# A longformer attention and softplus-MLP kernel: the planner's rules for queue, ring, port and fetch, and a new order

## The chip, the cores and the metric

The kernel runs on one core of a Trainium2 chip. The metric is device time in microseconds (us). Five engines work side by side and meet only at semaphores: TensorE (PE: matmuls; PEld is its weight load), VectorE (DVE), ScalarE (ACT), GpSimd (POOL) and SyncE (SP, which only issues transfers here). GpSimd issues transfers too, on a queue of its own.

## What is computed

Attention over 8 batches of 8 heads, 576 positions and 64 features, where a position sees its neighbours within 32 and 8 global positions; then, on the 4608 rows of 512 features, a layer of 2048 with softplus and a layer back to 512.

```python
scores = scale * np.matmul(q, k.transpose(0, 1, 3, 2))
mask = np.abs(pos[:, None] - pos[None, :]) <= 32
mask = mask | is_global[:, None] | is_global[None, :]
scores = np.where(mask, scores, -1e9)
attn = np.exp(scores - np.max(scores, axis=-1, keepdims=True))
attn = attn / (np.sum(attn, axis=-1, keepdims=True) + 1e-09)
x = np.matmul(attn, v).transpose(0, 2, 1, 3).reshape(4608, 512)
h = x @ w_in                      # 512 x 2048
g = np.maximum(h, 0.0) + np.log1p(np.exp(-np.abs(h)))
out = g @ w_out                   # 2048 x 512
```

## The kernel before

**The work.** The 4608 rows are nine tiles of 512. A tile is four groups of 128 positions ("pairs" n in the code). For each group TensorE makes the scores `s` (L1105), DVE adds the mask and takes the maximum (`st`, `m`, L1109 and L1122), GpSimd subtracts it (`st`, L1128), ACT takes the exponential (L1145), DVE sums and inverts (`sm`, `rs`, L1152 and L1154), GpSimd multiplies (`pn`, L1160), DVE transposes (`pt`, L1169), and TensorE multiplies with the values (`xo`, L1271). The first four groups take a shorter path, whose mask TensorE adds. The result is copied to `xT`, and the two layers follow: `h` (L1308, with weights `win`), softplus to `g` (L1314, ACT), and `o` (L1319, with weights `wout`), copied to `osb` and stored. Global rows of a batch go a way of their own: scores `sg` (L1003), maximum `gm` and `gnb` on DVE, exponential `pg` on ACT (L1015), transposed `pgt` (L1019, L1020), `ov` (L1029) on TensorE, then `odd`, `grs` and `vg`, which `xo` needs. `fill` copies a batch's global keys into `kx` (L755, `kx<-qkg`). The transposes of a later batch are `qx` (L859) and `kx` (L863). The first tile is cut into pieces of 128, 256 and 128 rows, the second into 128 and 384.

**The order.** Nothing in the program is in the order in which the code names it. Every step is a job with a cost on each engine that may do it, and `_Order.run` takes the jobs in the order that the table `ORDER` lists (a number is five times the job's number, plus its engine). The table so fixes which engine does a job and what stands in an engine's queue before what. The planner's own times decide two things more: how many filler matmuls `warm` (L762) are put on TensorE where it is planned to wait in the first 34 us (`keep`), and which PSUM bank a result takes. Each engine works off its queue in that order, and a step at the head that waits holds all behind it.

**The queues.** SP issues the loads of q and k, GpSimd those of `vb` (rounded values, 16 transfers), `win` (two to each of four tiles) and `wout` (four). SP's loads for batch 1 stand behind a tiny transfer, `trail<-win` (L789), which waits until the third tile of `win` has landed; those for batch 2 stand behind `trail<-wout`. GpSimd reads one element of the second half of batch 1's k (`seen`, L1454) before it issues `wout`, and issues batch 1's `vb` behind that.

**What the planner knows.** `stall` models TensorE's instructions as blocks of 256, asked for some 282 instructions before they are needed; `comes` says when such a block arrives. A job with `port` isn't put on DVE while GpSimd works on data, nor the other way round.

Of the kernel before, what the change touches and what calls it, by code (L numbers as in the profile page):

```python
# [19 lines left out]
class _Order:  # L20
# [20 lines left out]
    QUIET = 5000  # L41
    NEAR = 150

    def comes(self, here):

        t = here + self.QUIET
        for mine, start, moves, j in self.dma:
            if mine == "POOL" and j["at"] <= here + 300:
                t = max(t, min(j["end"] + 2300, here + 9300))
        return t  # L50

    def stall(self, t, took, ins):

        held, n = 0, self.issued
        asked, need, due, last = self.fetch
        due = list(due)
        while n + ins >= min(asked, need):
            at = min(asked, need)
            here = t + held + took * max(at - n, 0) / max(ins, 1)
            if at == asked:  # L60
                last = max(self.comes(here), last + self.FETCH)
                due.append(last)
                asked += self.BLOCK
            else:
                held += max(0, due.pop(0) - here)
                need += self.BLOCK
        return held, (asked, need, due, last)

    def add(self, cost, emit, deps=(), rank=5, opens=(), uses=(), table=None, moves=0, array=128, urgent=False, ins=None, late=0, hold=0, behind=(), lead=0, port=False):

        job = dict(cost=cost, emit=emit, deps=[d for d in deps if d is not None], rank=rank, opens=list(opens),
                   table=table, moves=moves, array=array, urgent=urgent, ins=ins, late=late, hold=hold, lead=lead, port=port, behind=[d for d in behind if d is not None], n=len(self.jobs), at=None, end=None)
# [91 lines left out]

    def size(self, j):
        return j["ins"] or 2
# [38 lines left out]
    def run(self, free):  # L205
# [13 lines left out]
        self.mine, self.other = [], []  # L219
        self.fetch, self.issued = (self.ASK, self.NEED, [], 0), 0  # L220
        while ready:
# [6 lines left out]
            for j in self.picked(ready):  # L228
# [6 lines left out]
                for e in j["cost"] if not self.given else [self.given[0][1]]:  # L235
# [7 lines left out]
                    elif e == "DVE" and j["port"]:  # L243
                        for a, z in self.other[-4:]:
                            if a <= t + 100 and z > t:
                                t = self.freed(z) if (a, z) == self.other[-1] else z
                    elif e == "POOL" and not self.issue(j):
# [46 lines left out]
            j["on"] = e  # L294
            order.append(j)
# [17 lines left out]
def kernel(  # L313
# [455 lines left out]
    T = {}  # L769
# [725 lines left out]
```

## Time and profile before

| | |
|---|---|
| median of 3 runs | 329.61 us (329.25 to 332.41) |
| the profiled execution | 331.38 us, of which the span of its instructions is 329.7 us |
| granted TensorE clock, mean | 0.99 |
| filler matmuls in the program | 34 |
| jobs on ACT, DVE, GpSimd | 364, 313, 143 |

A row of a timeline gives the start and length of an instruction or of several alike, the engine, the line, the operation with its tiles, and in brackets how long the engine had been idle before it and what ended that. "PEclk" is the granted clock of TensorE as a share of full speed. "issue" names a wait that nothing in the profile explains.

### The profile page before, as it was taken

What the parts mean: (1) busy time and instruction counts of PE and PEld (TensorE: products, weight loads), DVE (VectorE), ACT (ScalarE), POOL (GpSimd) and SP (SyncE); (2) the same over time, 40 slices, a digit from 0 to 9 for tenths busy, and PEclk for the clock granted to TensorE, in tenths of its full rate; (3) what the DMA queues carried; (4) which work ended last, traced back from release to release, by engine and by line L of the source; (5) the groups of instructions that cost most, each with busy time, mean ns of one, the idle gap of its engine ahead of it and who ended that gap; (6) DMA issues with size and microseconds to landing.
All of it is one profiled execution on the core that took longest, in us unless ns stands there. A gap on an engine that the chain in (4) does not pass through costs nothing.

```text
span 329.7 us, 11617 instructions
## 1 busy us (share of the span) xinstructions
PE 313.2 (95%) x5018; PEld 172.4 (52%) x5061; DVE 230.2 (70%) x410; ACT 224.9 (68%) x458; POOL 199.7 (61%) x180
## 2 busy tenths in 40 slices
PE   8879999699999998999999999999999999999996
PEld 3448974266557554544454455444544544454453
DVE  7876786974899999988985787599749727450000
ACT  7969844577589897398648972877569746934432
POOL 8984737977399377578768952949585604740000
PEclk9998999989999999999999999999999999999999
DMA  8999999995988999979990997403320002001002
GB/s 210 170 178 242 176 196 141 189 216 137 155 129 140 198 179 180 174 158 143 180 207 34 188 151 161 105 2 74 130 97 0 36 2 97 1 34 66 32 16 111
DMA packets 168651, 41.50 MB, mean 126 GB/s; under 512 B 153114, under 2 KB 165658, under 8 KB 168602
## 3 DMA queue, kind: packets, MB, share of 16 engines
q1 hardware_dynamic: 151048, 25.96, 44.7%
q0 software_dynamic: 15680, 11.67, 20.3%
q10 hardware_dynamic: 1874, 3.15, 2.5%
q8 instruction: 39, 0.64, 0.8%
q14 instruction: 10, 0.08, 0.1%
HBM read 36.70 MB, written 9.44 MB: 140 GB/s over the span
## 4 chain that ended last, share of the span: by engine, by line
PE 80%; DMA 9%; DVE 4%; issue 2%; POOL 2%; ACT 2%; SPq 0%
PE h L1308 34%; PE o L1319 33%; DMA stage<-in_k_dram 5%; PE xo L1271 4%; DMA wout<-in_moe_w_out_dram 4%; PE s L1105 3%; PE ov L1029 2%; POOL st L1128 1%; ACT st L1141 1%; PE pick L919 1%; PE warm L762 1%; PE sg L1003 1%; DVE sm L1152 1%; DVE kx L755 1%; POOL wout L1375 1%
## 5 line engine op out<-in xcount | busy, mean ns | idle before, releaser
L1308 PE MATMUL h<-xT,win 128*128 128x512 bf16 (+3 forms) x823 | 136.3, 314 | 1.2 <-issue 0.5
L1319 PE MATMUL o<-wout,g 128*128 128x512 bf16 (+1 forms) x563 | 131.0, 375 | 2.8 <-issue 2.4
L1314 ACT ACTIVATE g<-h 128x512 bf16<-128x512 f32 (+3 forms) x208 | 85.3, 481 | 37.5 <-PE h L1308 36.1
L1308 PEld LDWEIGHTS <-win 128*128 128x128 bf16 x832 | 70.7, 98 | 56.0 <-issue 1.2
L1160 POOL TENSOR_TENSOR pn<-st,rs 128x1024 bf16<-128x1024 f32 (+1 forms) x39 | 67.9, 1746 | 42.5 <-DVE rs L1154 38.8
L1319 PEld LDWEIGHTS <-g 128*128 128x128 bf16 x592 | 56.4, 98 | 62.0 <-issue 2.0
L1128 POOL TENSOR_TENSOR st<-st,m 128x1024 f32<-128x1024 f32 x32 | 60.3, 1897 | 24.7 <-DVE m L1122 23.9
L1109 DVE TENSOR_TENSOR st<-s,mask 128x512 f32<-128x512 f32 x64 | 41.1, 678 | 13.3 <-PE s L1105 13.3
L1152 DVE TENSOR_REDUCE sm<-st 128x8 f32<-128x1024 f32 x32 | 38.3, 1198 | 11.5 <-ACT st L1145 11.2
L1122 DVE TENSOR_REDUCE m<-st 128x8 f32<-128x1024 f32 x32 | 38.1, 1204 | 0.2
L1145 ACT ACTIVATE st<-st 128x1024 f32<-128x1024 f32 x32 | 32.9, 1055 | 5.2 <-POOL st L1128 5.0
L755 ACT COPY osb<-o 128x512 f32<-128x512 f32 (+1 forms) x26 | 14.9, 574 | 23.9 <-PE o L1319 21.6
L1169 DVE STREAM_TRANSPOSE pt<-pn 128x512 int32<-128x512 int32 x36 | 24.7, 690 | 2.8 <-POOL pn L1160 2.8
L755 DVE CAST xT<-xo 128x512 bf16<-128x512 f32 (+3 forms) x28 | 13.4, 524 | 15.9 <-PE xo L1271 15.8
L755 ACT CAST xT<-xo 128x512 bf16<-128x512 f32 (+3 forms) x24 | 9.8, 454 | 15.9 <-PE xo L1271 15.3
L1314 ACT ACT_TABLE_LOAD x13 | 16.7, 1283 | 3.0 <-PE h L1308 2.8
L1105 PE MATMUL s<-kx,qx 64*32 64x128 bf16 x1152 | 14.5, 220 | 2.4 <-DVE kx L863 1.3
L1105 PEld LDWEIGHTS <-qx 64*32 64x32 bf16 x1152 | 10.5, 90 | 10.4 <-issue 8.1
L1145 ACT ACT_TABLE_LOAD x12 | 15.4, 1283 | 0.6 <-ACT osb L755 0.4
L477 POOL DMA_DIRECT2D vb<-in_v_dram x16 | 11.1, 706 | 7.6 <-DMA wout<-in_moe_w_out_dram 7.5
L1331 POOL DMA_DIRECT2D out_dram<-osb x24 | 13.6, 569 | 3.3 <-DVE osb L755 2.2
L752 POOL TENSOR_SCALAR qk<-stage 128x1152 bf16<-128x1152 f32 (+1 forms) x9 | 12.5, 1394 | 3.6 <-PE h L1308 3.6
(129 smaller groups left out, 299.0 us busy)
## 6 DMA issues: line engine op xcount, KB each, us to landing
stage<-in_k_dram SPq DMA_DIRECT2D x48, 144.0 KB, 4.0
stage<-in_q_dram SPq DMA_DIRECT2D x48, 144.0 KB, 3.7
stage<-in_v_dram SPq DMA_DIRECT2D x48, 144.0 KB, 3.6
out_dram<-osb POOLq DMA_DIRECT2D x24, 256.0 KB, 3.0
out_dram<-osb ACTq DMA_DIRECT2D x11, 256.0 KB, 2.0
stage<-in_q_dram SPq DMA_DIRECT2D x4, 512.0 KB, 7.0
stage<-in_k_dram SPq DMA_DIRECT2D x4, 512.0 KB, 7.5
win<-in_moe_w_in_dram POOLq DMA_DIRECT2D x8, 256.0 KB, 6.5
```

The source lines that it names most:

```text
L755: {"ACT": nc.scalar.copy, "DVE": V.tensor_copy, "POOL": nc.gpsimd.tensor_copy}[e](out, in_)
L1105: nc.tensor.matmul(out=PS["s", n, g][quad(a), x, :], lhsT=qx[b % 2][rows(g), a, j * BL:(j + 1) * BL], rhs=kx[b % 2][rows(g), a, e0 * BL:(e ...
L1109: V.tensor_tensor(out=PS["st", n][:, h, :, :], in0=PS["s", n, h][:, :, :], in1=mask[:, h, j0:j0 + PB, :, :].rearrange("p j s i -> p j (s i ...
L1122: V.reduce_max(out=m[:], in_=flat(PS["st", n], h0, h1), axis=AX)
L1128: on(e).tensor_tensor(out=t, in0=t, in1=over(PS["m", n, y][:], SL * BL), op=OP.subtract)
L1145: nc.scalar.activation(out=t, in_=t, func=AF.Exp)
L1152: V.reduce_sum(out=sm[:], in_=flat(PS["st", n], h0, h1), axis=AX)
L1160: on(e).tensor_tensor(out=PS["pn", n][:, :, :, h0:h1].rearrange("p x s h -> p h x s"), in0=PS["st", n][:, h0:h1], in1=PS["rs", n, y][:].re ...
L1169: V.transpose(out=bass.AP(base.tensor, base.offset, ap=[list(base.ap[0]), [2 * STEP, PB // 2], [STEP + BL // 2, 2], [1, SL * BL]]), in_=PS ...
L1308: nc.tensor.matmul(out=h[:, :], lhsT=w_in_t[c // 4][:, kd, c % 4 * P:(c % 4 + 1) * P], rhs=PS["xT", m][:, kd, lo:hi], start=(kd == 0), sto ...
L1314: nc.scalar.activation(out=PS["g", m, c][:, lo:hi], in_=PS[key][:, lo_of(c, hi - lo)], func=AF.Softplus)
L1319: nc.tensor.matmul(out=PS["o", m, ns, a][:, :], lhsT=PS["g", m, kf][:, ns * P:(ns + 1) * P], rhs=w_out_t[kf // 4][:, kf % 4, a:z], start=( ...
```

## The change

Five rules of the planner, and with them a new table.

- Block arrival: `comes` and its constant 5000 ns go; a block asked for before a planned 13 us takes 6300 ns, then 7300, 9000, 6500, 8500 and 5000 (`SLOW`).
- GpSimd's queue: a job says how many transfers it sends (`sent`), and `ring` plans the ninth transfer not before the first of the eight ahead of it has landed.
- First transfers: batch 0's other parts are planned behind the first (`behind`), and the third and fourth tile of `win` 3700 and 3500 ns after the one before (`hold`).
- One more `port` operation: `fill` of batches 2 and later.
- `ORDER` is replaced in whole.

```diff
-    QUIET = 5000
+    SLOW = ((13000, 6300), (18000, 7300), (24000, 9000), (36000, 6500), (52000, 8500), (1e9, 5000))
-                last = max(self.comes(here), last + self.FETCH)
+                last = max(here + next(took for until, took in self.SLOW if here < until), last + self.FETCH)
+    QUEUE = 8
+    def ring(self, j, t):
+        n = len(self.sent)
+        for x in range(j["sent"]):
+            if n + x >= self.QUEUE:
+                d, back = self.sent[n + x - self.QUEUE]
+                t = max(t, d["end"] - back + 290 - 680 * x)
+        return t
...
+                    elif e == "POOL" and j["sent"]:
+                        t = self.ring(j, t)
...
-                                    rank=-1 if x else 0, hold=0, moves=2900 if x else 3500)
+                                    rank=-1 if x else 0, hold=(0, 0, 3700, 3500)[x], moves=2900 if x else 3500, sent=2)
...
-                             rank=rank - 1 if b else 0, uses=[kkey] if early else [], lead=0 if b else LEAD)
+                             rank=rank - 1 if b else 0, uses=[kkey] if early else [], lead=0 if b else LEAD, port=not early)
...
-        52, 126, 4, 57, 102, 62, 147, 65, 106, 141, 116, 201, 132, 72, 205, 217, 136, 9, 152, 212, 232, 157, 122, 14,
...
+        8820, 8826,
```

The program itself gets no rule of its own from the first four: its transfers, semaphores and instructions are the same, but for four more filler matmuls (38), and jobs that change engine. ACT has now 370 jobs, DVE 305, GpSimd 145. Lines move down by 7 or 8, so that `fill` and the other copies, L755, are now L762, and L1128 is L1136.

GpSimd's queue around the loads of `win`, before:

```order
L477 DMA vb_67<-in_v_dram 32x18x64 x8
L1371 DMA win_130<-in_moe_w_in_dram 64x4x512 x2
L1371 DMA win_131<-in_moe_w_in_dram 64x4x512 x2
L1160 TENSOR_TENSOR pn<-st,rs 128x512
L1371 DMA win_132<-in_moe_w_in_dram 64x4x512 x2
L1160 TENSOR_TENSOR pn<-st,rs 128x512 x4
L1371 DMA win_133<-in_moe_w_in_dram 64x4x512 x2
L699 COPY mask<-mask 128x2x256
```

and now, where the copy of the mask and the clearing of batch 1's tiles stand ahead of the third tile, and the fourth directly behind it; two casts of batch 0 also stand ahead of the first `vb` now:

```order
L484 DMA vb_67<-in_v_dram 32x18x64 x8
L1379 DMA win_130<-in_moe_w_in_dram 64x4x512 x2
L1379 DMA win_131<-in_moe_w_in_dram 64x4x512 x2
L706 COPY mask<-mask 128x2x256
L558 MEMSET kx_72 128x40x16
L558 MEMSET kx_72 128x4x16 x2
L558 MEMSET qkg_74 128x64
L584 MEMSET vb_68 128x18x2
L1168 TENSOR_TENSOR pn<-st,rs 128x512
L1379 DMA win_132<-in_moe_w_in_dram 64x4x512 x2
L1379 DMA win_133<-in_moe_w_in_dram 64x4x512 x2
L1168 TENSOR_TENSOR pn<-st,rs 128x512 x4
```

Around `wout`, the same queue had one cast of k shortly ahead of `seen` and nothing between `seen` and the first `wout`; now two such casts stand ahead of `seen` and two more between it and `wout`. The four `wout`, eight `vb` and four `st` behind them are as they were, in the same order. On SP's queue the loads of batch 1 were, behind the little transfer:

```order
L789 DMA trail<-win_132 1x2x1
L532 DMA stage_60<-in_q_dram 128x8x128
L532 DMA stage_61<-in_k_dram 128x8x128 x2
L532 DMA stage_60<-in_q_dram 128x8x128
L536 DMA stage_60<-in_q_dram 64x4x64 x2
```

and are now (`stage_60` is q, `stage_61` is k):

```order
L796 DMA trail<-win_132 1x2x1
L539 DMA stage_61<-in_k_dram 128x8x128 x2
L539 DMA stage_60<-in_q_dram 128x8x128 x2
L543 DMA stage_61<-in_k_dram 64x4x64 x2
L543 DMA stage_60<-in_q_dram 64x4x64 x2
```

Both of k's large loads come ahead of q's now. DVE's queue around batch 1's global row, between the last maxima of its first groups and `pgt`, before:

```order
L1122 TENSOR_REDUCE m<-st 128x8 x2
L1152 TENSOR_REDUCE sm<-st 128x8
L1154 RECIPROCAL rs<-sm 128x8
L1009 TENSOR_REDUCE gm<-sg 128x1 x2
L1010 TENSOR_REDUCE gnb<-gm 128x1
L1109 TENSOR_TENSOR st<-s,mask 128x512 x2
L1152 TENSOR_REDUCE sm<-st 128x8
L1154 RECIPROCAL rs<-sm 128x8
L1019 STREAM_TRANSPOSE pgt<-pg 128x576
L1020 TENSOR_REDUCE pgt<-own 128x18x8
```

and now, with one sum instead of two ahead of `pgt`, and `gm` ahead of both:

```order
L1130 TENSOR_REDUCE m<-st 128x8 x2
L1017 TENSOR_REDUCE gm<-sg 128x1 x2
L1018 TENSOR_REDUCE gnb<-gm 128x1
L1117 TENSOR_TENSOR st<-s,mask 128x512 x2
L1160 TENSOR_REDUCE sm<-st 128x8
L1162 RECIPROCAL rs<-sm 128x8
L1027 STREAM_TRANSPOSE pgt<-pg 128x576
L1028 TENSOR_REDUCE pgt<-own 128x18x8
```

ACT, which took three exponentials ahead of `pg`, takes two now. On TensorE thirteen fillers stand now ahead of the first `xo`, where there was none, and the four fillers between its `heat` matmuls (L768) and the first `h` are gone; up to batch 1's `ov` it has 49 `o` matmuls instead of 53. The `fill` of batch 4 moves from DVE to ACT: before, DVE had

```order
L1109 TENSOR_TENSOR st<-s,mask 128x512
L859 STREAM_TRANSPOSE qx_69<-qk 128x1152
L938 STREAM_TRANSPOSE qkg_73<-placed 128x256
L755 COPY kx_71<-qkg_73 128x40x8
L863 STREAM_TRANSPOSE kx_71<-qk 128x4x9x32
L1169 STREAM_TRANSPOSE pt<-pn 128x2x2x128
```

and now ACT has it behind a table load and an exponential:

```order
L762 COPY odd<-ov 64x129 x2
L1153 ACT_TABLE_LOAD
L1153 ACTIVATE st<-st 128x1024
L762 COPY kx_71<-qkg_73 128x40x8
L1048 ACTIVATE vg_76<-odd,grs 128x128
```

The fills of batches 2 and 5 move to ACT as well, those of 6 and 7 to DVE.

More of the change, by code (lines that the diff above doesn't have):

```diff
@@ L40 @@
     FETCH = 4000
-    QUIET = 5000
+    SLOW = ((13000, 6300), (18000, 7300), (24000, 9000), (36000, 6500), (52000, 8500), (1e9, 5000))
     NEAR = 150
[L44 to L50, printed above, removed]
     def stall(self, t, took, ins):
@@ L67, in stall, with add @@
         return held, (asked, need, due, last)
-    def add(self, cost, emit, deps=(), rank=5, opens=(), uses=(), table=None, moves=0, array=128, urgent=False, ins=None, late=0, hold=0, behind=(), lead=0, port=False):
+    def add(self, cost, emit, deps=(), rank=5, opens=(), uses=(), table=None, moves=0, array=128, urgent=False, ins=None, late=0, hold=0, behind=(), lead=0, port=False, sent=0):
         job = dict(cost=cost, emit=emit, deps=[d for d in deps if d is not None], rank=rank, opens=list(opens),
-                   table=table, moves=moves, array=array, urgent=urgent, ins=ins, late=late, hold=hold, lead=lead, port=port, behind=[d for d in behind if d is not None], n=len(self.jobs), at=None, end=None)
+                   table=table, moves=moves, array=array, urgent=urgent, ins=ins, late=late, hold=hold, lead=lead, port=port, sent=sent, behind=[d for d in behind if d is not None], n=len(self.jobs), at=None, end=None)
         self.jobs.append(job)
@@ L218, in run @@
         dma = self.dma = []
-        self.mine, self.other = [], []
+        self.mine, self.other, self.sent = [], [], []
         self.fetch, self.issued = (self.ASK, self.NEED, [], 0), 0
@@ L294, in run @@
             j["on"] = e
+            for x in range(j["sent"]):
+                self.sent.append((j, j["moves"] / 2 if x + 1 < j["sent"] else 0))
             order.append(j)
@@ L794, in add_rounded @@
             T["cast", b, 2].append(o.add({"POOL": (1360, 0)}, lambda e, c=c: load_rounded(b, c), T["cast", b, 2][-1:] or deps,
-                                         rank=-1, moves=1250, hold=0))
+                                         rank=-1, moves=1250, hold=0, sent=2))
         T["load", b, 2] = T["cast", b, 2][-1]
@@ L822, in add_parts @@
             T["part", b, w, t] = o.add({"DMA": (700 if b else 0, 0)}, emit, had(("w_in", 2)) + T["cast", 0, w] if b else [], rank=0,
-                                       moves=(1740 if b else 1830) if t < FULL else 900 if b else 670)
+                                       moves=(1740 if b else 1830) if t < FULL else 900 if b else 670,
+                                       behind=had(("part", 0, 0, 0)) if not b and x else [])
     def add_cast(b, w):
@@ L1365, in add_moe @@
             if m < OWN:
-                o.add({"POOL": (700, 2700)}, lambda e, ns=ns: store(nc.gpsimd, ns, 0, d_model), [T["oev", m, ns]], rank=-0.5, hold=0, port=2,
+                o.add({"POOL": (700, 2700)}, lambda e, ns=ns: store(nc.gpsimd, ns, 0, d_model), [T["oev", m, ns]], rank=-0.5, hold=0, port=2, sent=1,
                       uses=[("osb", m, ns)])
@@ L1456 @@
                 T["w_out", a] = o.add({"POOL": (800, 0)}, lambda e, a=a: weights_out(a),
-                                      [T["landed"], T.get(("w_out", a - 1))], rank=-1, hold=0, moves=2560)
+                                      [T["landed"], T.get(("w_out", a - 1))], rank=-1, hold=0, moves=2560, sent=1)
         for x in range(len(VALS)):
```

147 rows, old and new, of the table ORDER are left out of this document.

## The prediction

> **What bounds the kernel now.** I read the page first, then the busy time by stretches, then the timelines of the engines at the two places where TensorE stands still.
>
> ```profile
> span 329.7 us, 11617 instructions
> PE 313.2 (95%) x5018; PEld 172.4 (52%) x5061; DVE 230.2 (70%) x410; ACT 224.9 (68%) x458; POOL 199.7 (61%) x180
> ```
>
> TensorE is the bound over the whole: idle for 16.5 us of 329.7. An average hides where, so these stretches are cut at its waits:
>
> ```profile
> core 0: us, PE busy (x) PEld busy (x) DVE busy (x) ACT busy (x) POOL busy (x), PEclk, DMA share, GB/s
> 21.66:23.17 1.51, 0.26 (x7) 0.12 (x8) 1.20 (x3) 0.04 (x1) 1.34 (x2) 1.00 1.24 200
> 23.17:27.00 3.83, 3.61 (x57) 2.43 (x58) 2.17 (x6) 2.72 (x16) 1.79 (x4) 0.55 0.82 116
> 27.00:60.15 33.15, 32.48 (x645) 23.66 (x645) 24.81 (x54) 22.39 (x70) 20.68 (x27) 1.00 1.23 191
> 60.15:63.01 2.86, 0.00 (x1) 0.00 (x1) 2.79 (x6) 1.70 (x3) 2.84 (x3) 1.00 1.09 183
> 64.01:68.00 3.99, 3.66 (x72) 1.66 (x73) 2.84 (x9) 1.91 (x7) 3.84 (x4) 0.57 1.11 206
> 68.00:131.20 63.20, 61.42 (x1144) 37.73 (x1151) 55.70 (x84) 52.13 (x107) 45.06 (x32) 1.00 0.93 164
> 131.20:326.60 195.40, 192.58 (x2687) 96.50 (x2711) 121.55 (x191) 124.25 (x191) 104.01 (x71) 1.00 0.42 92
> ```
>
> After 131.2 us TensorE is busy for 192.58 of 195.40: a new order can win at most 2.8 us there. Two waits cost more than themselves, because the granted clock falls behind them, to 0.55 over 3.83 us and to 0.57 over 3.99 us, that is, (1 - 0.57) x 3.99 = 1.7 us each. The work of TensorE around the waits:
>
> ```profile
> 21.01 0.42 PE L1105 MATMUL s<-kx,qx 64*32 64x128 bf16 x32
> ...
> 23.17 0.21 PE L1271 MATMUL xo<-pt,vg 32*64 32x128 bf16 x1 [1.26 <-issue]
> ...
> 23.64 1.03 PE L768 MATMUL xo<-idle 128*128 128x256 bf16 x4
> ...
> 26.18 2.06 PE L1308 MATMUL h<-xT,win 128*128 128x128 bf16 x28
> ...
> 49.24 5.56 PE L1319 MATMUL o<-wout,g 128*128 128x512 bf16 x25
> ...
> 63.01 0.80 PE L1029 MATMUL ov<-vb,pgt 32*32 32x129 bf16 x72 [2.86 <-DVE pgt L1020]
> ...
> 66.64 0.28 PE L1271 MATMUL xo<-pt,vg 32*64 32x64 bf16 x8
> ...
> 74.05 0.38 PE L1271 MATMUL xo<-pt,vg 32*64 32x384 bf16 x8
> ```
>
> So there are three sizes to argue about: when the first `h` starts (26.18), the wait of `ov` at 60.15 with the slow clock behind it (2.86 + 1.7 = 4.6 us), and one later wait:
>
> ```profile
> 131.60 0.42 PE L1105 MATMUL s<-kx,qx 64*32 64x128 bf16 x32 [1.28 <-DVE kx L863]
> ```
>
> **The first h.** The third group of scores ended at 21.01 + 0.42 = 21.43 before. Now the three fillers between the halves of the first `ov` (0.75 us) are gone, so it ends at about 20.8; thirteen fillers at 5.56/25 = 0.22 us take 2.9, and `xo` starts at 23.7, after the 23.17 at which its wait with no releaser ended. With `xo` (0.5), `heat` at full clock (0.5) and the copies to `xT` (0.5) `h` can start at 25.2. At worst the unexplained wait comes late too, and `h` starts at 26.2 as before. I take 25.6, between them, and save a further (1 - 0.55) x 0.8 = 0.4 us, since 26.18 to 27 ran at the slow clock and TensorE now has no idle time ahead.
>
> **TensorE's way to ov.** From 26.18 to 60.15 it took 33.97 us. Now 4 `o` are fewer (-0.9), two fillers more (+0.4), the slow clock gone (-0.4): 33.1. It reaches `ov` at 25.6 + 33.1 = 58.7, or at 59.5 from the late end.
>
> **What ov waits for.** Its `pgt` hangs on GpSimd's queue:
>
> ```profile
> POOL vb L477 <- DMA wout<-in_moe_w_out_dram: 7.5, 4, 2.7
> 16.59 1.27 POOL L1371 DMA_DIRECT2D win<-in_moe_w_in_dram  x2
> ...
> 22.81 1.27 POOL L1371 DMA_DIRECT2D win<-in_moe_w_in_dram  x2
> ...
> 33.12 0.61 POOL L755 CAST qk<-stage 128x512 bf16<-128x512 f32 x1 [1.15 <-PE h L1308]
> ...
> 36.09 3.10 POOL L1375 DMA_DIRECT2D wout<-in_moe_w_out_dram  x4
> ...
> 51.53 0.66 POOL L477 DMA_DIRECT2D vb<-in_v_dram  x1 [2.75 <-DMA wout<-in_moe_w_out_dram]
> 52.20 7.46 POOL L1128 TENSOR_TENSOR st<-st,m 128x1024 f32<-128x1024 f32 x4
> ```
>
> The last four of the eight `vb` waited 7.5 us, each for one of the four `wout` to land: eight transfers stand open, and a ninth holds GpSimd. The change alters nothing in that; `wout`, `vb` and the `st` behind them keep their order. Call T0 the end of the last `vb` issue, 52.19 before. Behind T0:
>
> ```profile
> 55.99 1.06 ACT L1145 ACTIVATE st<-st 128x1024 f32<-128x1024 f32 x1 [0.79 <-POOL st L1128]
> ...
> 59.53 0.89 ACT L1015 ACTIVATE pg<-sg,gnb 128x320 bf16<-128x320 f32 x2 [0.63 <-DVE gnb L1010]
> ...
> 65.17 0.40 ACT L1040 ACTIVATE vg<-odd,grs 128x128 bf16<-128x128 f32 x1
> 57.08 1.22 DVE L1152 TENSOR_REDUCE sm<-st 128x8 f32<-128x1024 f32 x1 [3.13 <-ACT st L1145]
> ...
> 58.45 0.77 DVE L1009 TENSOR_REDUCE gm<-sg 128x1 f32<-128x320 f32 x2
> ...
> 61.89 0.73 DVE L1019 STREAM_TRANSPOSE pgt<-pg 128x576 bf16<-128x576 bf16 x1
> 62.65 0.30 DVE L1020 TENSOR_REDUCE pgt<-own 128x144 bf16<-128x144 bf16 x1
> ```
>
> Before, `pgt` was done at 62.95, T0 + 10.8, because `gm` stood behind a sum that waited 3.13 us for an exponential, and `pgt` behind a second. Now `gm` is ahead of both. Two `st` (7.46/4 = 1.87 each), the second exponential (1.06) and `pg` (0.89) give T0 + 5.7; one sum with its inverse (1.4) beside that, from T0 + 4.8 at the latest, gives T0 + 6.2; `pgt` (1.05) is done at T0 + 7.3. This saves 3.5 us if T0 stands.
>
> T0 moves by three things. The third `win` stands behind two casts (2 x 0.61) and the copy and clearings, so it is issued up to 2.5 us later, and the loads of batch 1 wait for it:
>
> ```profile
> 24.12 0.73 SPq L789 DMA_DIRECT2D trail<-win  x1
> ...
> 25.47 3.89 SPq L532 DMA_DIRECT2D stage<-in_k_dram  x2
> GB/s 205 238 182 207 197 207 143 80 59 66 152 117 139 191 197 189 265 321 325 307 296 289 290 323 274 289 298 300 299 213 200 195 134 80 94 64 86 139 174 195
> ```
>
> The last row is what all queues moved from 20 to 40 us, in slices of 0.5. The `win` in hand moved at some 200 GB/s up to 23 us without a gap, so the third tile's landing should move by the casts' 1.2 us alone (bounds 0 and 2.5). k's second load goes second instead of third: at the row's 300 GB/s one load's 512 KB is worth 1.7 us, and up to 4.5 if neither load of q and only half of the fourth `win`, issued at 22.81 before, share its time any more. I take 3.1, the middle. Two casts of k between `seen` and `wout` add 1.2. Sum: +1.2 - 3.1 + 1.2 = -0.7, so T0 is 51.5, with ends at 48.9 and 54.2. `pgt` is then done at 58.8 (56.2 to 61.5), and `ov` starts at 59.0, 4.0 us earlier than 63.01, with so short a wait that the clock holds.
>
> **From ov to 74.** `ov` (0.8) and eight `o` (1.8) bring TensorE to `xo` at 61.6; its `vg` needs `pt` of the first group, at T0 + 7.46 + 1.9 + 0.7, and then `odd`, `grs` and `vg` (0.9): T0 + 11.0 = 62.5. Before, 66.64: 4.1 earlier. The next `xo` (74.05) needs GpSimd's nine operations behind T0, 9 x 1.88 = 16.9, and a transpose and copy on DVE behind: T0 + 18.7 = 70.2. TensorE itself, with the 7.4 us that lay between 66.64 and 74.05 (less 0.4 of slow clock, one `o` more), comes at 62.5 + 7.2 = 69.7. I take 70.5: 3.5 us are won here, of 1.2 (T0 at 54.2) to 4.3.
>
> **The wait at 131.6.** Here lies the fourth rule of the change:
>
> ```profile
> 83.83 0.24 DVE L755 COPY kx<-qkg 128x320 bf16<-128x320 bf16 x1
> ...
> 127.91 2.34 DVE L755 COPY kx<-qkg 128x320 bf16<-128x320 bf16 x1
> 130.18 1.37 DVE L863 STREAM_TRANSPOSE kx<-qk 128x1152 int32<-128x1152 int32 x1
> 126.41 3.74 POOL L1160 TENSOR_TENSOR pn<-st,rs 128x1024 bf16<-128x1024 f32 x2
> ```
>
> The same `fill` took 0.24 us with GpSimd idle and 2.34 under two `pn`, and it ended with them, at 130.2. The new order gives it to ACT and so takes 2.1 us from DVE ahead of the `kx` that TensorE waited 1.28 for. On ACT it stands behind a table load and an exponential of 1.06, so part may come back: I take 0.9 won, of 0 to 1.28. Under "SBUF: two separate sides" the Trainium skill's page "SBUF — State Buffer" says that GpSimd also shuts out DVE operations with two SBUF inputs. By that the one `pn` of 128x1024 that moves to DVE could wait a whole GpSimd operation; no row here shows one, and the sum holds nothing for it.
>
> **The sum.** 3.5 + 0.9 = 4.4 us. The profiled execution took 331.38 us, 1.68 more than its span, so it would take 327.0. The median of the runs is 1.77 below it: 329.61 - 4.4 = **325.2 us**. I put the later tiles at nothing, since TensorE's work there is the same matmuls; their waits come under the third rival. About 1% is what a measurement of this kernel can tell: 326.3 and 332.9 are the bounds.
>
> **Rivals.** First, GpSimd's queue is as late as its late end (the plan respects eight open transfers, but removes none). With T0 at 54.2, `pgt` is done at 61.5, TensorE waits 2.8 us from 58.7, and the `xo` of 74.05 starts at 54.2 + 18.7 = 72.9 or, if the clock falls again for 1.7, at 54.2 + 11.0 + 7.2 + 1.7 = 74.1. Then 0 to 1.2, and 0.9 at 131.6, are won: 328.1. The longer queue ahead of the third `win` speaks for it, k's order against it. Chance 0.2. By the Trainium skill's "TensorE: Matmul & The Clock Gate", under "What's actually happening", the clock falls after an idle window of some 3.4 us, so that a wait of 2.8 would not cost it, and this rival would end at 327.5. The trace differs: it fell behind waits of 1.51 and 2.86 us, so I keep the price.
>
> Second, DVE takes the gain back. It is busy 55.70 of 63.20 us from 68 to 131.2, and if its work can't start earlier TensorE runs into it at the first `xo` of a whole tile, as at 131.6. Only about 1 us stays: 328.6. Against it: its sums follow T0, which moves, and the fills leave it. Chance 0.15.
>
> Third, slower: DVE's transposes `pt` come late for the `xo` of tiles 3 to 8, which the new order puts elsewhere among the `o`. One wait of 1.28 at each of six, as at 131.6, is 7.7, less 4.4: 332.9. Two waits above 1.5 us with 1.7 of slow clock each already take all of the gain. For it: the order is new in all of them, and the wait at 131.6 arose so. Against it: only 2.8 us were idle in the old order's 195. Chance 0.15.
>
> **Chances and range.** My forecast has 0.5, with its own range 322.5 to 327.2 (T0's ends, and up to 1 us won or lost after 131). A tenth of it lies above 326.3; the first two rivals lie within 1%, the third half within. So faster 0.46, same 0.41, slower 0.13. The range goes from 322.2 to 331.5, into the third rival.
>
> **What would show it.** Right: first `h` at 25 to 26 with a clock of 1.00 before it; `pgt` done 7 to 8 us behind the last `vb` issue; less than 1 us of idle time ahead of batch 1's `ov`, and no slow clock behind it; the `xo` of 128x384 at 70 to 71; no wait of `s` on `kx` in batch 4. Wrong: a last `vb` issue after 53 us, a new wait above 1.5 us with the clock down behind it, or DVE named ahead of `xo` in the later tiles.

## The result, and the profile after

| | before | after |
|---|---|---|
| median beside each other, 20 runs each | 329.81 us (328.65 to 332.41) | 328.13 us (326.16 to 330.93) |
| ratio, 95% interval | | 0.9937 [0.9913, 0.9961] |
| the profiled execution, its span | 331.38 us, 329.7 us | 329.9 us, 328.2 us |
| runs with a mean granted clock below 0.998, of all whose clock is listed, later sets included | 69 of 98 | 10 of 38 |

The change wins 1.7 us, about 0.6%, where 4.4 were forecast: the median is 2.9 us above the forecast of 325.2. Four runs of later sets (331.50, 366.86, 455.59 and 803.75 us) are slow ones, and no ratio below counts them.

The profile after, busy time by stretches (same columns as in the prediction):

```profile
27.00:60.00 33.00, 30.89 (x625) 22.30 (x623) 24.09 (x51) 20.21 (x64) 19.08 (x22) 0.95 1.28 195
60.00:68.00 8.00, 8.00 (x180) 4.44 (x179) 7.86 (x14) 5.53 (x12) 6.42 (x4) 1.00 0.93 147
68.00:131.20 63.20, 63.20 (x1179) 37.66 (x1177) 56.20 (x88) 52.18 (x109) 47.20 (x36) 1.00 0.95 183
...
46.00:50.00 4.00, 4.00 (x43) 1.64 (x43) 2.78 (x5) 0.73 (x5) 0.66 (x1) 0.57 1.67 183
```

From 60 to 131.2 us TensorE has no idle time at all: the waits of 2.86 ahead of `ov` and of 1.28 ahead of batch 4's `s` are gone, and so is the slow clock behind `ov`. But the loss has moved forward: idle time and a stretch of slow clock (0.57 on average from 46 to 50) now lie between 27 and 60. TensorE's timeline there:

```profile
23.27 0.40 PE L1279 MATMUL xo<-pt,vg 32*64 32x128 bf16 x8
...
26.09 2.84 PE L1316 MATMUL h<-xT,win 128*128 128x128 bf16 x48 [1.56 <-DVE xT L762]
...
44.52 0.31 PE L898 MATMUL tr<-ident,qk 64*64 64x64 bf16 x8 [1.57 <-DVE qk L757]
...
63.03 0.80 PE L1037 MATMUL ov<-vb,pgt 32*32 32x129 bf16 x72
...
65.59 0.23 PE L1279 MATMUL xo<-pt,vg 32*64 32x64 bf16 x8
...
73.56 0.38 PE L1279 MATMUL xo<-pt,vg 32*64 32x384 bf16 x8
```

`ov` starts when it did before (63.01), without a wait: TensorE itself came late. GpSimd's queue and DVE say why the chain behind it was no faster:

```profile
34.77 3.17 POOL L1383 DMA_DIRECT2D wout<-in_moe_w_out_dram  x4
...
50.05 0.66 POOL L484 DMA_DIRECT2D vb<-in_v_dram  x1 [2.08 <-DMA wout<-in_moe_w_out_dram]
...
22.77 1.94 DVE L1168 TENSOR_TENSOR pn<-st,rs 128x512 bf16<-128x512 f32 x1
...
44.17 0.29 DVE L757 TENSOR_SCALAR qk<-stage 128x256 bf16<-128x256 f32 x1 [4.00 <-DMA stage<-in_q_dram]
...
51.33 2.48 DVE L1117 TENSOR_TENSOR st<-s,mask 128x512 f32<-128x512 f32 x4 [2.07 <-PE s L1113]
...
62.62 0.30 DVE L1028 TENSOR_REDUCE pgt<-own 128x144 bf16<-128x144 bf16 x1
```

T0, the end of the last `vb` issue, is 50.71, as forecast (51.5). But `pgt` is done at 62.92, T0 + 12.2 and not T0 + 7.3: DVE stood 2.07 us for scores of TensorE, TensorE had stood 1.57 us for a cast of q, and DVE 4.00 us for the last of batch 1's loads of q, which that cast reads. Behind that wait TensorE's clock was slow, so the eight `o` ahead of those scores took 3.39 us, and 1.90 in a later profile at full clock. And the first `h` waited for copies that stand on DVE behind a `pn` of 1.94 us, where the same operation takes 0.70 elsewhere.

### The profile page after: what moved, and what is told of

Its sections match the earlier page's. It is cut to its first block, busy times and chain, and to the rows that moved or that the text cites. A ratio compares the mean times of both kernels' runs of the same rounds, so it can differ in the third digit from the quotient of the medians.

```text
span 328.2 us, 11662 instructions
## 1 busy us (share of the span) xinstructions
PE 317.9 (97%) x5065; PEld 171.0 (52%) x5065; DVE 226.3 (69%) x402; ACT 232.2 (71%) x468; POOL 200.2 (61%) x182
## 3 DMA queue, kind: packets, MB, share of 16 engines
q1 hardware_dynamic: 151048, 25.96, 44.2%
## 4 chain that ended last, share of the span: by engine, by line
PE 87%; DVE 4%; DMA 4%; SPq 1%; POOL 1%; ACT 1%; issue 0%; ACTq 0%; DVEq 0%; POOLq 0%
PE o L1327 39%; PE h L1316 36%; PE xo L1279 4%; DMA stage<-in_q_dram 4%; PE s L1113 4%; PE ov L1037 2%; SPq L543 1%; DVE m L1128 1%; PE pick L927 1%; PE sg L1011 1%; DVE pn L1168 1%; DVE qx L762 0%; ACT osb L762 0%; PE tr L895 0%; POOL near L666 0%
## 5 line engine op out<-in xcount | busy, mean ns | idle before, releaser
L1327 PE MATMUL o<-wout,g 128*128 128x512 bf16 (+1 forms) x592 | 139.8, 377 | 0.0
L1316 PEld LDWEIGHTS <-win 128*128 128x128 bf16 x832 | 70.8, 98 | 59.5 <-issue 3.2
L1136 POOL TENSOR_TENSOR st<-st,m 128x1024 f32<-128x1024 f32 x32 | 60.5, 1895 | 42.8 <-DVE m L1130 42.5
L1168 POOL TENSOR_TENSOR pn<-st,rs 128x1024 bf16<-128x1024 f32 (+1 forms) x36 | 64.4, 1797 | 24.8 <-DVE rs L1162 15.1
L762 ACT CAST xT<-xo 128x512 bf16<-128x512 f32 (+3 forms) x30 | 12.2, 468 | 21.0 <-PE xo L1279 20.9
L762 ACT COPY osb<-o 128x512 f32<-128x512 f32 (+1 forms) x30 | 17.2, 572 | 11.4 <-PE o L1327 9.9
L762 DVE CAST xT<-xo 128x512 bf16<-128x512 f32 (+3 forms) x22 | 10.6, 514 | 7.2 <-PE xo L1279 7.2
L762 POOL CAST vb<-stage 128x1152 bf16<-128x1152 f32 x12 | 13.7, 1152 | 1.9 <-PE xo L1279 1.0
```

The costliest lines, as they stand in the source:

```text
L762: {"ACT": nc.scalar.copy, "DVE": V.tensor_copy, "POOL": nc.gpsimd.tensor_copy}[e](out, in_)
L1136: on(e).tensor_tensor(out=t, in0=t, in1=over(PS["m", n, y][:], SL * BL), op=OP.subtract)
L1168: on(e).tensor_tensor(out=PS["pn", n][:, :, :, h0:h1].rearrange("p x s h -> p h x s"), in0=PS["st", n][:, h0:h1], in1=PS["rs", n, y][:].re ...
L1316: nc.tensor.matmul(out=h[:, :], lhsT=w_in_t[c // 4][:, kd, c % 4 * P:(c % 4 + 1) * P], rhs=PS["xT", m][:, kd, lo:hi], start=(kd == 0), sto ...
L1327: nc.tensor.matmul(out=PS["o", m, ns, a][:, :], lhsT=PS["g", m, kf][:, ns * P:(ns + 1) * P], rhs=w_out_t[kf // 4][:, kf % 4, a:z], start=( ...
```

## The experiments

The three readings to start with: L, batch 1's last loads land late and hold the scores on which `pgt` hangs; X, the first copies are late, through the `pn` that moved to DVE; V, the loads land when the transfer queues have got through their volume, whatever is issued first. Ratios are to runs of the kernel before on the same chip in the same sitting; differences below 0.4% or so can't be told in one set.

**The changed kernel again, and three edits of its first 30 us.** First, nothing changed.

> The changed kernel once more, to see a second execution in profile. Theory L (late loads): the profiled execution of it lost 1.57 us at the transposes of batch 1's last q rows, and 1.7 us of slow clock behind that, because those two small loads landed at 44.1, among the packets of wout. Where they land a little earlier the clock holds at 1.00, and the span is near 326. Theory X (first copies): the loss is the same in each execution, namely the 1.56 us ahead of the first h, and the wait ahead of batch 1's last transposes is there in this one too. Both: ratio to before 0.990 to 0.997.

0.9945 [0.9917, 0.9973]. The profiled execution had a span of 327.0 and was another one: the last q load was cast at 41.88 and `tr` no longer waited for it, but now the clock was at 0.57 on average from 26 to 30 us, behind the wait of the first `h`. `ov` started at 61.85.

Then the third `win` directly behind the second:

```diff
 DMA win_131<-in_moe_w_in_dram 64x4x512 x2
+DMA win_132<-in_moe_w_in_dram 64x4x512 x2
 COPY mask<-mask 128x2x256
...
-DMA win_132<-in_moe_w_in_dram 64x4x512 x2
```

> One move in the changed kernel: GpSimd issues the third win tile directly behind the second, ahead of the mask's copy, five clearings and one pn; fillers held at the changed kernel's counts. L: the tile lands 1 to 1.5 us earlier (trail's issue at 24.3 to 24.8 instead of 25.8), so do batch 1's loads, the last q rows are there before 43, the wait of 1.57 us is under 0.5 and the clock 1.00; 1 to 2.5 us faster than the changed kernel, ratio to before 0.986 to 0.991. Rival V (the queue's volume alone sets when the tile lands): trail's issue stays within 0.4 of 25.8, and the ratio stays at 0.994. X: no faster than the changed kernel, since the pn that waits for it makes xT later still.

0.994 [0.991, 0.9971]. The third tile was issued some 2.6 us earlier and nothing came of it: the little transfer that waits for its landing was issued at 25.96 (25.77 in the profile after), the last q load was cast at 43.74. The issue of that tile doesn't set its landing, as V has it. The landing did move with the change, by 1.65 us (the little transfer came at 24.12 before), near the prediction's 1.2: the first two tiles too are issued 1.8 us later, at 14.62 instead of 12.80, which fits, but no run takes it apart.

Then the one `pn` back from DVE to GpSimd:

```diff
 DVE: RECIPROCAL rs<-sm 128x4
-DVE: TENSOR_TENSOR pn<-st,rs 128x512
 DVE: TENSOR_REDUCE m<-s 128x4
...
-POOL: TENSOR_TENSOR pn<-st,rs 128x512 x4
+POOL: TENSOR_TENSOR pn<-st,rs 128x512 x5
```

> One pn of the second group goes from DVE (where it took 1.94 us beside GpSimd's pn) back to GpSimd; fillers as in the changed kernel. X: xT is copied 1.3 us earlier, the first h starts at 24.6 to 25.0 instead of 26.09, and the kernel is 1.0 to 1.5 us faster (ratio to before 0.989 to 0.991). L: the first h starts earlier too, but TensorE then waits as much longer for batch 1's loads, whose time is unchanged; ratio within 0.002 of the changed kernel's.

0.9941 [0.9914, 0.9969], and none of its 12 runs had a mean clock below 0.998. TensorE's timeline of it:

```profile
24.95 1.28 PE L1318 MATMUL h<-xT,win 128*128 128x128 bf16 x20 [0.48 <-DVE xT L764]
27.10 1.72 PE L1318 MATMUL h<-xT,win 128*128 128x128 bf16 x28 [0.88 <-DMA win<-in_moe_w_in_dram]
...
43.68 0.31 PE L900 MATMUL tr<-ident,qk 64*64 64x64 bf16 x8 [0.98 <-DVE qk L759]
...
60.56 0.80 PE L1039 MATMUL ov<-vb,pgt 32*32 32x129 bf16 x72
```

X was right of the first `h`: 24.95 instead of 26.09. But it then waited 0.88 for `win` and 0.98 for q, and the median is that of the changed kernel: in this profile, what one step earns the next loads take.

Both edits together:

> Both moves together. L and X both in part right: the gains add, 2 to 3.5 us faster than the changed kernel, ratio to before 0.983 to 0.988. L alone: as with the earlier win tile alone. X alone: as with the pn alone.

0.9961 [0.9926, 0.9996], no better. In the profiled execution the other moved `pn` on DVE fell beside GpSimd's two, and the first `xo` waited 2.22 us for it:

```profile
21.22 3.47 DVE L1170 TENSOR_TENSOR pn<-st,rs 128x512 bf16<-128x512 f32 x1
21.95 2.15 POOL L1170 TENSOR_TENSOR pn<-st,rs 128x512 bf16<-128x512 f32 x2
25.56 0.26 PE L1281 MATMUL xo<-pt,vg 32*64 32x128 bf16 x8 [2.22 <-DVE rs L1164]
```

**Each of the two terms alone, in the kernel before.** `gm` ahead of the sums on DVE, `pg` behind two exponentials on ACT:

```diff
 TENSOR_REDUCE m<-st 128x8 x2
-TENSOR_REDUCE sm<-st 128x8
-RECIPROCAL rs<-sm 128x4
 TENSOR_REDUCE gm<-sg 128x1 x2
...
 TENSOR_REDUCE pgt<-own 128x18x8
+TENSOR_REDUCE sm<-st 128x8
+RECIPROCAL rs<-sm 128x4
```

> The kernel before, with one part of the new order alone: batch 1's gm and gnb stand ahead of the sums on DVE, and pg behind two exponentials on ACT instead of three. Theory P (the prediction's step, pgt hangs on the end of GpSimd's vb issues, T0): T0 stays near 52.2, pgt is done at T0 + 7.3 = 59.5 instead of T0 + 10.8, TensorE waits less than 0.5 us at ov (2.86 before), and the xo of 128x384 starts 2.5 to 3.5 us earlier; the median falls by 2.5 to 3.5 us, to some 327. Theory G (the gain is given back): ov starts earlier all the same, but the xo of 128x384 is held by pn and pt and starts after 73; the median falls by less than 1 us. Theory C (part of the forecast gain was slow clock, which only some executions have): ov's wait goes, and the median falls by 1.5 to 2.5 us.

0.9956 [0.9938, 0.9974], 1.5 us (1.8 between the medians), and one run of 12 with a lower clock. Its DVE and TensorE:

```profile
54.67 0.43 PE L1003 MATMUL sg<-kx,qkg 128*32 128x320 bf16 x8
55.04 0.82 DVE L1009 TENSOR_REDUCE gm<-sg 128x1 f32<-128x320 f32 x2 [1.15 <-PE sg L1003]
...
59.29 0.30 DVE L1020 TENSOR_REDUCE pgt<-own 128x144 bf16<-128x144 bf16 x1
60.02 0.80 PE L1029 MATMUL ov<-vb,pgt 32*32 32x129 bf16 x72
...
71.14 0.38 PE L1271 MATMUL xo<-pt,vg 32*64 32x384 bf16 x8
```

T0 is 51.61 here, `pgt` is done at 59.59, T0 + 8.0, and the waits for `pgt` come to 0.4 us in all. `ov` and the `xo` of 128x384 start 3.0 and 2.9 us earlier than in the profile before. So P's times of `ov` and `xo` came true, G fell, and C held of the size: 2.9 between two executions, 1.5 to 1.8 in the median. But `pgt` doesn't hang on T0 here, and that it came near P's 59.5 is luck: `gm` stood 1.15 us for TensorE's scores `sg`, and `pgt` is done 4.92 us behind the start of `sg`, here and in two later runs with other T0 (below).

Batch 4's `fill` alone, from DVE to ACT:

```diff
 DVE: STREAM_TRANSPOSE qkg_73<-placed 128x256
-DVE: COPY kx_71<-qkg_73 128x40x8
 DVE: STREAM_TRANSPOSE kx_71<-qk 128x4x9x32
...
 ACT: ACTIVATE g_2961<-h 128x384
+ACT: COPY kx_71<-qkg_73 128x40x8
 ACT: ACT_TABLE_LOAD
```

> The kernel before, with only batch 4's fill moved from DVE to ACT. The prediction's term: 0.9 us won, of 0 to 1.28: the wait of s on kx at 131.6 falls below 0.4 us, and the time from ov to the end (266.7 in the profile before, 265.2 in that after) falls to some 265.6. Rival: fill waits on ACT behind the table load and the exponential of 1.06, kx is as late as before, and the median stays within 0.3 us.

0.9973 [0.9949, 0.9998], 0.9 us. The stretch from the `xo` of 128x384 to that of 192 in batch 4, which holds the wait, falls from 62.32 to 61.00 us. This run also shows what the kernel before does up to 70 us with the clock at 1.00 throughout, since nothing differs until there:

```profile
24.99 1.73 PE L1308 MATMUL h<-xT,win 128*128 128x128 bf16 x28
...
62.47 0.80 PE L1029 MATMUL ov<-vb,pgt 32*32 32x129 bf16 x72 [2.15 <-DVE pgt L1020]
...
72.22 0.38 PE L1271 MATMUL xo<-pt,vg 32*64 32x384 bf16 x8
...
133.22 0.29 PE L1271 MATMUL xo<-pt,vg 32*64 32x192 bf16 x8
```

The first `h` comes 1.2 us earlier than in the profile before, the `xo` of 128x384 1.8, and a wait of 2.15 us ahead of `ov` left the clock alone.

**T0 and the loads, in the changed kernel.** Two of batch 1's `vb` ahead of `wout`, then four (and the `pn` on GpSimd):

```diff
+DMA vb_68<-in_v_dram 32x18x64 x2
 DMA wout_134<-in_moe_w_out_dram 128x4x512
...
-DMA vb_68<-in_v_dram 32x18x64 x8
+DMA vb_68<-in_v_dram 32x18x64 x6
```

> The changed kernel, with two of batch 1's eight vb transfers issued ahead of wout instead of behind it, so that wout is issued 1.3 us later, behind the last two q loads. Theory L (TensorE's way to ov is the predicted 33.1 us, but it stands still for batch 1's last q loads, which land late among wout's packets, and pgt hangs on the scores behind them): the last q load lands by 42.5, the wait of tr near 44 falls from 1.57 to under 0.4 us, ov starts near 60.5 at full clock, and the median falls by 0.6 to 1.2 us against the changed kernel's 328.2; T0 falls by 4 us or so, as two waits for wout go, and that alone gives nothing. Theory Q (GpSimd's queue): pgt follows T0, is done 4 us earlier, and ov starts when TensorE comes. Theory W: the first o (45.6) waits for wout, landing 1.3 us later, and nothing is won or up to 1.5 us lost.

> The changed kernel with four of batch 1's vb transfers ahead of wout, and the one pn back on GpSimd. Theory L with the first copies: the first h starts at 25.0, tr waits for no load, ov starts near 59.5, and the span is 324.6, the median 326.3 to 326.8. Theory W: wout, issued 2.6 us later, lands after the first o needs it at 45.6; a wait of 1 to 2 us appears ahead of o and the median stays at 328.

0.9948 [0.9922, 0.9975] and 0.9981 [0.9952, 1.001]. T0 fell to 48.04 and 43.20, `pgt` was done at 60.86 and 60.66: Q fell, T0 is not what it hangs on in this order. The last `tr` waits no more, as L has it, but it didn't in the second profile of the changed kernel above either, so this is not shown to come from the edit. W held as well: `o` now waits for `wout` at 47.14 (0.35 us), and with four `vb` ahead twice, 0.27 and 0.73. A second wait shows in both:

```profile
90.16 1.52 POOL L761 TENSOR_SCALAR qk<-stage 128x1152 bf16<-128x1152 f32 x1 [2.94 <-DMA stage<-in_v_dram]
...
101.95 0.38 PE L1281 MATMUL xo<-pt,vg 32*64 32x384 bf16 x8 [1.09 <-ACT vg L1050]
```

In the first of them, GpSimd stands 2.94 us for a load of a later batch, its `st` and the exponentials behind it are late, and at the end `vg`. In the second it stands 2.71, and `xo` 0.86. The same wait for `vg` is in the profiles of the run with the third `win` earlier (1.04, behind 2.91 on GpSimd) and of the one with `fill` back on DVE, below (0.73, behind 2.57); in the other profiles of this order GpSimd stands there 0.81 us at most, and `xo` not at all.

Three of the four transfers of `wout` left out, so that the output is another (and the `pn` on GpSimd):

```diff
     def weights_out(a):
+        if a:
+            return
```

> The changed kernel with the one pn back on GpSimd, and three of the four transfers of wout left out: every o multiplies with the first quarter of w_out, so the output is another. Theory B (batch 1's loads of q and wout share engines that are full from 23 to 50 us, and a later wout only moves the wait to o): the last q load lands before 42.5, the wait of tr near 44 (0.98 us in the run with the pn alone) goes without another in its place, ov starts at 59.4 to 59.8 (60.56 there), and the span is 324.6 to 325.0. Rival R (the small q loads are slow for their 256-byte packets alone): they land at 43.3 as before, and ov starts at 60.5.

0.9855 [0.9828, 0.9882], by far the lowest, and all five runs at a clock of 0.999 or more. The last q load was cast at 41.73, as B has it, but an execution with all of `wout` also came to 41.88, so this doesn't tell B from R; and 0.69 us ahead of an `h` at 41.28, for which the profile names no releaser, took part of it back (`ov` at 60.13). Against the same kernel with all of `wout` (0.9941, on another chip) the missing 1.5 MB are worth 0.9%, nearly 3 us, though the profiled execution (span 325.3) is no better than the lowest run with all of it (325.0). What they buy is that the executions are alike: 325.94 to 327.02 us, where that kernel's went from 326.73 to 330.49.

**What the rest of the change is worth.** `fill` back on DVE in the changed kernel:

> The changed kernel with batch 4's fill back on DVE. If the fourth rule's edit is worth in the new order what it was worth in the old one (the stretch from the xo of 128x384 to that of 192 fell from 62.32 to 61.00 us there), the stretch grows from 60.7 to 62.0, a wait of some 1.3 us comes back ahead of batch 4's s, and the median rises by 1.0 to 1.3 us to 329.4. Rival: the other parts of the new order around batch 4 took that wait away, the stretch stays at 60.7, and the median is within 0.4 us of the changed kernel's 328.2.

0.9939 [0.9912, 0.9966], the changed kernel's ratio: the rival held of the median. The stretch, though, is 62.32 us long, as the first theory had it. Of this 0.73 is the wait for `vg`, which makes the stretch 62.0 to 62.2 with `fill` on ACT too, and some 0.4 is left for `fill` (without that wait the stretch is 61.6, and 61.1 to 61.2 in those): most of it a wait of 0.34 ahead of batch 4's `s`, not 1.3. The copy stood behind both transposes here, with no GpSimd operation beside it, and took a tenth of its time in the profile before:

```profile
125.30 1.34 DVE L873 STREAM_TRANSPOSE kx<-qk 128x1152 int32<-128x1152 int32 x1
126.56 0.67 DVE L1179 STREAM_TRANSPOSE pt<-pn 128x512 int32<-128x512 int32 x1
127.15 0.20 DVE L764 COPY kx<-qkg 128x320 bf16<-128x320 bf16 x1
127.50 0.42 PE L1115 MATMUL s<-kx,qx 64*32 64x128 bf16 x32 [0.34 <-DVE kx L764]
```

Then the two edits together in the kernel before, and with two `vb` ahead of `wout`:

> The kernel before with both edits: gm ahead of the sums, and batch 4's fill on ACT; the four other rules' moves left out. If these two are all that the new order wins, 1.8 and 1.0 us add up to 2.8, and the median is 327.5, at or below the changed kernel's 328.2: the moved first transfers then gave nothing, or cost a little. Rival: the two gains overlap (DVE's work ahead of batch 4 starts earlier anyway), the median is 328.5, and the changed kernel's other moves are worth something.

> As the one before, and two of batch 1's eight vb transfers ahead of wout. There T0 is what pgt hangs on (T0 + 8.0, ov waited 0.4 us), so T0 falls by 3 to 4 us, ov no longer waits, and the xo of 128x384, which came 11.1 us behind ov there, comes 9.8 behind (as where ov was late): 1 to 1.7 us more, median 326 to 326.5. Rival: a load of batch 2 comes late for GpSimd's cast at 90, vg late for the xo near 101, and 1 us of it is lost again: 327.2. Second rival: wout, 1.3 us later, holds the first o.

0.9891 [0.9864, 0.9919] and 0.9897 [0.9869, 0.9924]. The two edits at least add up. A T0 3.5 us earlier (47.57) adds nothing even here, and the median of 327.79 misses the 326 to 326.5 expected: `pgt` was done at 59.76, 4.92 us behind `sg` again (59.15 in the run without the moved `vb`, also 4.92), and TensorE came at 60.19 and waited for no one. Last, that kernel beside the changed one:

> The changed kernel unchanged, beside the next run on one chip. Theory M (the moved first transfers and copies cost about 1 us, and gm and fill alone carry the gain): its median lies 0.6 to 1.3 us above that of the kernel before with gm and fill alone. Rival: the two are the same kernel in time, within 0.4 us, and the moved transfers cost nothing.

> The kernel before with gm ahead of the sums and batch 4's fill on ACT, again. Theory M: 327.2 to 327.6 where the kernel before is at 330.2, 0.6 to 1.3 us below the changed kernel; fewer than one run in four with a mean clock below 0.997, as its wait at ov is 0.4 us or less. Rival: within 0.4 us of the changed kernel, near 328.2.

0.9909 [0.9873, 0.9945] and 0.9897 [0.9866, 0.9929], medians 327.57 and 327.52 us. M's 0.6 to 1.3 us don't show, as far as six runs each can tell: two moves in the table earn about what the whole new order earns, and the moved first transfers neither cost nor give what can be told. Two of the six runs of the last kernel had a mean clock below 0.997, where fewer than one in four was expected. The changed kernel's profiled execution here is the one without the late load of q, the slow clock and the wait for `vg`:

```profile
25.29 1.28 PE L1316 MATMUL h<-xT,win 128*128 128x128 bf16 x20 [0.47 <-DVE xT L762]
27.53 1.72 PE L1316 MATMUL h<-xT,win 128*128 128x128 bf16 x28 [0.96 <-DMA win<-in_moe_w_in_dram]
...
59.78 0.80 PE L1037 MATMUL ov<-vb,pgt 32*32 32x129 bf16 x72
...
70.31 0.38 PE L1279 MATMUL xo<-pt,vg 32*64 32x384 bf16 x8
```

The other kernel's profile has a late T0, 53.60, and there `pgt` does hang on it, by the prediction's own chain: the sum stands for an exponential behind T0, and `pgt` is done at 60.93, T0 + 7.3.

```profile
58.49 1.22 DVE L1152 TENSOR_REDUCE sm<-st 128x8 f32<-128x1024 f32 x1 [0.32 <-ACT st L1145]
...
60.63 0.30 DVE L1020 TENSOR_REDUCE pgt<-own 128x144 bf16<-128x144 bf16 x1
```

## Why the prediction missed the size, and where it held

**The step that failed is the one from the profile to the median**: "The median of the runs is 1.77 below it: 329.61 - 4.4". The 4.4 us were found in an execution with two stretches of slow clock: in the prediction's own terms 2.1 us of TensorE's time (0.4 ahead of `h` and 1.7 behind `ov`) are that clock. Only 6 of 98 runs of the kernel before have a mean clock as low as the profiled 0.990; 63 lie from 0.993 to 0.995 and 29 at 0.998 or more, with median spans of 330.15, 328.9 and 327.6 us. One stretch takes 0.005 off the mean (half the clock for 3.4 of 329 us, see the last section), so the median run of before had one of them, not two. Of the 4.4 us, the 1.77 by which the profiled execution was slower than the median (1.3 of it the second stretch) were already gone from the time that they were taken off. In the run with the `fill` alone, the old order at full clock has the `xo` of 128x384 at 72.22 instead of 74.05: 1.8 of the 3.5 us forecast there belonged to that execution.

Like with like, at a clock of 0.998 or more, the spans fall from 327.6 to 326.0 us: 1.6. Besides, fewer runs have a slow stretch (10 of 38 instead of 69 of 98), which at some 1.5 us a stretch (1.3 between those spans of before, 1.8 in after) is worth 0.44 x 1.5 = 0.7. Together 2.3, about what the three sets of the changed kernel show (0.6 to 0.9%). Another 0.3 lies outside the spans (time less span is 1.99 us at the median of those 98 runs and 1.72 of those 38), for which the profile shows no cause.

The forecast of one execution, 327.0 us with the `xo` at 70.5, came out in the best of the three profiled ones (326.65 and 70.31; the others took 329.90 and 328.76), and only 6 of the 38 runs take 327.0 or less. So of the 2.9 us by which the median missed, 1.8 is the step above, some 0.7 lies between 327.0 and the 327.7 of a run at full clock (span 326.0 and 1.7), through what follows, and 0.4 is the slow stretch that a quarter of the runs keep.

**What ov waits for.** The reading of the wait of 2.86 us held: with `gm` ahead of the sums it is gone. "`pgt` is done at T0 + 7.3" is one of two chains, and the prediction put the other, from TensorE's scores, at nothing. In the old order with `gm` moved, `pgt` was done at T0 + 7.3 in one of four profiles and 4.92 us behind `sg` in three. In the new order it follows the four DVE `st` that stand a few rows ahead of `gm` (51.33 in the profile after) by a fixed time, in which DVE has work throughout, and these wait for TensorE's scores.

| changed kernel, with edits | T0 | the `st` start | `pgt` done |
|---|---|---|---|
| as it is | 50.71 | 51.33 | 62.92 |
| as it is, last time | 50.64 | 48.09 | 59.67 |
| two `vb` ahead | 48.04 | 49.28 | 60.86 |
| four `vb` ahead, `pn` on GpSimd | 43.20 | 49.07 | 60.66 |

The last two columns stand 11.6 us apart in every row; T0 moves over 7.5 us without effect. Once the sums no longer stood between T0 and `pgt`, the scores were what came last. I had asked what is late next only of GpSimd and of TensorE's count of matmuls.

**TensorE's way to ov**, 33.1 us, was right as work: in the last profile 59.78 - 25.29 = 34.49, of which 0.96 and 0.24 are waits, leaves 33.3. Missing was any idle time in it. The kernel before had only 0.7 us there, and I carried that over, although the change brings `wout` 1.3 us forward (34.77, from 36.09), ahead of the last q loads, and puts a cast of q last among batch 1's. That the load is late is shown; that `wout` makes it late is not (below).

**The first h** was put at 25.6; it is 24.8 to 25.3 where the moved `pn` takes 0.70 to 0.83 us or is given back to GpSimd, and 26.1 where it takes 1.86 or 1.94 (27.16 in the run with both edits, where the other `pn` took 3.47). The Trainium skill's page "SBUF — State Buffer" ("SBUF: two separate sides"), that GpSimd shuts out DVE operations with two SBUF inputs, was quoted under the wait at 131.6 and left out of the sum. The runs agree with it: a DVE `pn` of 128x512 took 0.70 us by itself and 1.32, 1.94 and 3.47 as it fell beside GpSimd's. The prediction named the wrong operation for it, the `pn` of 128x1024 (1.29 us in the profile after); the short ones in the first tile carry the price.

**The wait at 131.6**, 0.9 us: right, by the mechanism named (0.0027 of 330 us), but in the new order `fill` is worth only some 0.4 us of it. **The later tiles at nothing**: TensorE's time from the `xo` of 192 in batch 4 to the end is 193.3 us in every profile of the old order and 193.9 in every one of the new, 0.6 lost.

**The rivals.** The first, a late T0, didn't occur. The second, that DVE takes the gain back, gives nearly the right number (328.6) by luck, since DVE is not named ahead of the `xo` of the later tiles. The third, late `pt` in tiles 3 to 8, didn't occur; the one late `xo`, at 101, waits for `vg` and costs about 1 us. As for the clock, neither rule holds as it was used: the Trainium skill's "TensorE: Matmul & The Clock Gate" ("What's actually happening") has an idle window of some 3.4 us, and the clock fell behind waits of 1.53 and 1.57 us; but it did not fall behind the 1.56 ahead of the first `h` in the profile after, nor behind 2.15 (ahead of `ov`) or 2.22 (ahead of the first `xo`), so my price of 1.7 us for each wait above 1.5 was no rule either. (The 1.51 that the prediction names is a stretch in which TensorE worked 0.26.) The last section shows most of what decides it.

Open is why the load that GpSimd waits for near 90 us lands late in some executions and not in others.

## What to carry to other kernels

Before the gain of one profiled execution is taken off a median, ask which parts of that execution the median run has: here one number per run, the mean clock, would have told. When a chain of waits is cut, follow all inputs of the thing that waited, not the one that ended last: the next one may be a load that nothing waited for so far. And try the two or three moves that carry the forecast in the old order first; here they earn about all that a new order of some 1800 entries does.

## Not expected of the hardware

How late the last q load lands goes with a few tenths of a microsecond of its issue. SP's queue and DVE's cast in the first and in the last profile of the changed kernel:

```profile
35.42 1.25 SPq L543 DMA_DIRECT2D stage<-in_q_dram  x2
```

```profile
34.40 1.25 SPq L543 DMA_DIRECT2D stage<-in_q_dram  x2
...
41.23 0.29 DVE L757 TENSOR_SCALAR qk<-stage 128x256 bf16<-128x256 f32 x1 [1.01 <-DMA stage<-in_q_dram]
```

So the issue ended at 36.67 and 35.65, and the casts began at 44.17 and 41.23. In the seven profiles in which the order of these transfers is that of the change (and all of `wout` is loaded):

| issue of the last two q loads ends | 35.65 | 35.77 | 35.95 | 36.23 | 36.35 | 36.41 | 36.67 |
|---|---|---|---|---|---|---|---|
| cast of the second starts | 41.23 | 42.20 | 41.88 | 43.02 | 43.33 | 43.74 | 44.17 |

One microsecond at the issue goes with three at the landing, with `wout` begun at 34.6 to 34.9 each time. That small loads on one queue share their time with large ones that get ahead of them on the other was my reading (L); the run without most of `wout` has 41.73 for an issue that ended at 35.94, near the table's own value, so `wout` alone is not what spreads it, and the cause stays open.

The slow clock keeps to a grid. The 0.55 and 0.57 above are averages over windows cut too wide: the clock is 0.50, for 3.41 us each time. In all 16 profiles the moments at which the granted clock changes lie whole multiples of 3.413 us apart, and where this grid lies against the kernel differs from execution to execution. So the right question is not how long one wait is, but how much idle time falls into one window of the grid. Such a window and the next, in the profile after, in the one of the changed kernel run again, and at `ov` in the profile before:

```profile
42.85:46.26 3.41, 1.84 (x64) 1.30 (x70) 2.06 (x7) 1.32 (x6) 0.66 (x1) 1.00 1.24 206
46.26:49.67 3.41, 3.41 (x40) 1.28 (x27) 2.52 (x4) 0.47 (x3) 0.66 (x1) 0.50 1.63 185
```

```profile
22.72:26.13 3.41, 1.88 (x58) 1.09 (x56) 3.19 (x8) 2.45 (x14) 1.37 (x2) 1.00 1.20 190
26.13:29.54 3.41, 3.41 (x34) 3.41 (x34) 2.12 (x4) 2.40 (x7) 1.77 (x2) 0.50 1.13 225
```

```profile
61.01:64.42 3.41, 1.25 (x75) 0.99 (x77) 3.34 (x6) 1.36 (x3) 3.26 (x4) 1.00 1.12 216
64.42:67.83 3.41, 3.08 (x71) 1.43 (x71) 2.26 (x7) 1.34 (x6) 3.39 (x3) 0.50 1.08 198
```

Of the 1495 whole windows in the 16 profiles, nine hold 1.49 us of idle time or more, and a window at 0.50 follows seven of them; none follows the others, with 1.46 or less. The wait of 1.56 in the profile after lay across a boundary (1.25 in one window), and so did the one of 2.22 (1.38 and 1.32). The two exceptions, the window with the wait of 2.15 ahead of `ov` (2.04 idle) and one of 1.52 near the end of the last profile of the changed kernel, stay open.
